# Block-sparse attention and a gated MLP: nine loads moved to GpSimd's queue, three transposes moved to the DMA, two weight transposes moved to later slots

## The chip, the cores and the metric

The kernel runs on one core of a Trainium2 chip. A core has five engines with a queue each: TensorE (PE) multiplies matrices, and its weight loads are listed apart as PEld; VectorE (DVE), ScalarE (ACT) and GpSimd (POOL) compute elementwise; SyncE (SP) issues transfers. Sixteen DMA engines move the data. TensorE writes to PSUM, and DVE or ACT take results from there to SBUF. Every engine works through its own instructions in order and waits on semaphores for the others. The metric is the device time of one execution in microseconds; given is the median of several runs.

## The reference

```python
# q, k, v: (4, 8, 768, 64); blocks of 32; window 1; first and last block global;
# three sampled blocks for each query block
scores = q @ k.T / sqrt(64)
scores = where(mask, scores, -1e9)
attn = softmax(scores)
x = (attn @ v), heads laid side by side            # (4, 768, 512)

h = relu(x @ w_in)                                 # (4, 768, 1024)
u, v = h[..., :512], h[..., 512:]
v_n = (v - mean(v)) / sqrt(var(v) + 1e-6)          # over the 512
v_s = einsum('ts,bsd->btd', w_spatial, v_n) + b_spatial
out = (u * v_s) @ w_out                            # (4, 768, 512)
```

Inputs and output are float32. The kernel computes in bfloat16 with float32 sums.

## The kernel before

Heads are taken in pairs: 16 pairs, four of them to a batch element. For a pair, k, q and v are loaded as float32 (`load`, line 105), cast to bfloat16 by POOL (`cast`, L138; k and q go into a tile `nat`, v into `vv`), and k and q are transposed. For pairs 0 to 3 PE transposes them; from pair 4 on SP issues one DMA transpose of the whole `nat` into `tt` (`tr_dma`, L448), and two DVE copies (`split`, L221, `kq<-tt`) bring the halves to the two heads' `kq`. The mask is part of the product: 24 more rows of `kq` hold one-hot blocks of keys and the bias of the query block.

Time is cut into slots, and the code at the end of the kernel (line 881 on) writes the order out by hand. In each slot PE computes one group of scores, ACT takes the exponential of it (L483 or L495), PE multiplies an earlier group with v, and then come the functions that are entered for this slot: `when(slot, ...)` enters them before the steps of the MLP, `late` behind these. Slots 0 to 35 do pairs 0 to 3 in thirds of the queries (`UNITS`, `qk_unit`, `av_unit`); from slot 36 on each slot is a sixth of one head (`qk_full`, `av_full`), so that a pair takes 12 slots, pair 4 from slot 36, pair 5 from 48, pair 6 from 60, pair 7 from 72.

The result of a unit is normalized by DVE (`normalize`, L506 and L507) into a tile `xn`. The MLP needs it transposed, `xt`. For pairs 0 to 3 `xtr_third` (line 564) does it third by third: two PE transposes (L308) into an unused part of the unit's own PSUM tile, and a DVE copy to `xt`. `XT_AT` gives the slots of these calls, otherwise 3u + 7 for unit u; units 8, 9, 10 and 11 are the last thirds of pairs 0 to 3. From pair 4 on a DMA transpose does it (`xtr_dma`, L573).

The MLP of a batch element is a list of steps, each one matmul of 512 columns (L621), dealt out over the slots by `run_queue` and the table `STEPS`: v and u products (x times `w_in`), s products (spatial weights times normalized v, evicted at L694), o products (times `w_out`). They write to two PSUM banks in turn. A v product is evicted by DVE (L188, `vn<-ps_moe`), its mean and variance taken by DVE (L657, L658), POOL makes `std` and `rstd` of a group (L661, L663), and DVE applies them (L188, `vn<-vn,mv,rstd`). In batch element 0 the groups are pairs of chunks: v0 and v1, v2 and v3, v4 and v5, and its v4 needs the last third of x of pairs 0 to 3, from slot 42 on.

The spatial weights are loaded by SP, cast by POOL in six parts at slots 19 to 29 (`ws_cast`, L589, into two buffers `ws_b`), and transposed by three DMA transposes (`ws_tr`, L593). `O_ACT` says which o products of each batch element ACT evicts and which DVE. SP's queue holds nearly all loads, stores and DMA transposes, in order.

Of the kernel before, what the change touches and what calls it, by code (L numbers as in the profile page):

```python
# [26 lines left out]
def kernel(  # L27
# [16 lines left out]
    nc = tc.nc  # L44
# [19 lines left out]
    TC = NCH // NT  # L64
    TW = TC * 128
# [152 lines left out]
    PL, DV = nc.gpsimd, nc.vector  # L218

    def dve_copy(o, i):  # L220
        nc.vector.tensor_copy(out=o, in_=i)  # L221
# [82 lines left out]
    def bank(nm="ps", tag=None):  # L304
        return psum.tile([128, 1024], BF16, tag=tag or moe_tag(), bufs=2 if tag else 1, name=nm)

    def tr(ps, c, in_):
        nc.tensor.transpose(out=ps[:, c * 128:(c + 1) * 128], in_=in_, identity=ident)  # L308

    def pair_of(src, c):  # L310
        return src[:, c].rearrange("p h d -> p (h d)")
# [143 lines left out]
    a_ref, av_ref, x_ref, xn_ref, xt_ref = {}, {}, {}, {}, {}  # L455
# [96 lines left out]
    def xt_tile(p):  # L552
        if p not in xt_ref:
            xt_ref[p] = work.tile([128, S], BF16, tag="xt", bufs=7, name="xt")
        return xt_ref[p]

    def xtr_pe(p, xn, c0, n, ps=None):
        if ps is None:
            ps = bank()
        for c in range(n):  # L560
            tr(ps, c, pair_of(xn, c))
        dve_copy(xt_tile(p)[:, c0 * 128:(c0 + n) * 128], ps[:, 0:n * 128])

    def xtr_third(u):
        t, p = UNITS[u]
        if t == "h":
            if p == 1:
                xtr_pe(0, xn_ref.pop(0), 0, 2 * TC)
        else:
            xtr_pe(p, xn_ref.pop(u), t * TC, TC, x_ref.pop(u))  # L570

# [54 lines left out]
        return out  # L626

    NORM_AT = {1: 23, 0: 23, 3: 36, 2: 36}
    O_ACT = [(4,), (0, 2, 4), (0, 2)]
    ST_ACT = [(), (), (4,), (0, 1, 2)]  # L630
    VN_AGE, VN_STEP = 9, 2
    post = []
# [1 line left out]
    class Moe:  # L634
# [75 lines left out]
        def o_product(self, tcc):  # L710
# [4 lines left out]
            for i in range(parts):  # L715
                cs = slice(i * w, (i + 1) * w)

                def done(ps, i=i, cs=cs):
                    if i == 0:
                        osb["t"] = work.tile([128, DM], FP32, tag="osb", bufs=6, name="osb")  # L720
                    on_act = (tcc + i) % 2 == 0 if self.last else tcc in O_ACT[self.b]
                    (act_copy if on_act else dve_copy)(osb["t"][:, cs], ps)
# [48 lines left out]
    def when(slot, *fns):  # L771
        at.setdefault(slot, []).extend(fns)

    def c(f, *a, **kw):
        return lambda: f(*a, **kw)
# [14 lines left out]
    when(2, staged)  # L790
    for p, sl in ((3, 18), (0, 21)):
        when(sl, c(tr_rest, p, 2 if p == 0 else 1))
    XT_AT = {1: 12, 3: 15, 5: 23, 11: 41}
    for u in range(1, len(UNITS)):
        late.setdefault(XT_AT.get(u, 3 * u + 7), []).append(c(xtr_third, u))
    late[12].append(c(tr_rest, 1))
# [54 lines left out]
    def slot_of(p):  # L851
        return S0 + 12 * (p - NG)

    for p in range(NG, NP):
        g = slot_of(p)
        when({4: 13, 5: 22, 6: 31}.get(p, g - 34), c(load, p, "k"), c(load, p, "q"), c(load, p, "v"))
        when({4: 18, 5: 26, 6: 38}.get(p, g - 24),
             c(cast, p, "k", PL), c(cast, p, "q", PL), c(cast, p, "v", PL))
        when({4: 20, 5: 31}.get(p, g - (16 if p in (10, 14) else 20)), c(tr_dma, p))
        when(31 if p == 4 else g - (7 if p in (9, 13) else 5), c(split, p, 0))  # L860
        when(32 if p == 4 else g - 3, c(split, p, 1))
        when(g + (18 if p == NP - 1 else 19 if p % NG == NG - 1 else 20), c(xtr_dma, p))
        if p == NP - 1:
            when(g + 20, last_x)
    for i, (ld, ca) in enumerate([(16, 19), (16, 21), (17, 23), (17, 25), (18, 27), (18, 29)]):
        if i < 5:
            when(ld, c(ws_load, i, 2 if i == 4 else 1))
        when(ca, c(ws_cast, i))
    for i, sl in enumerate((23, 27, 31)):
        when(sl, c(ws_tr, i))  # L870
    when(44, c(w_out_load, 0), c(w_out_load, 1), c(w_out_load2, 2))
    when(52, *[c(w_out_cast, g, PL) for g in range(NDH)])
# [58 lines left out]
```

## Time and profile before

| | |
|---|---|
| median of 3 runs | 208.85 us (208.24 to 209.13) |
| the profiled execution | 208.44 us, of which the span shown is 206.7 us |
| PE busy | 201.2 us |
| ACT busy | 166.8 us |
| DVE busy | 131.4 us |
| POOL busy | 74.4 us |
| moved by DMA | 42.41 MB, 205 GB/s |

A line of a timeline is: start, duration, engine, line and operation, output<-inputs, shapes, count, and in brackets the idle time of the engine just before it with what ended it. A line of the waits is: engine, line and output, what it waited for, total us, times, longest us. L12 is line 12 of the kernel. DMA-issuing instructions stand on the issuing engine with the time that the issue takes, and the time to landing counts from the issue. Times are microseconds from the start of the span.

### The profile page before, as it was taken

How to read it: one execution, taken by the hardware profiler on the slowest of the kernel's cores; microseconds unless marked ns; L12 is line 12 of the kernel's file. 1: busy time of each engine (PE TensorE's matmuls, PEld its weight loads, DVE VectorE, ACT ScalarE, POOL GpSimd, SP SyncE). 2: the span in 40 equal slices, each digit the busy share in tenths (PEclk: the TensorE clock that was granted, in tenths of full speed). 3: DMA queues.
4: the chain of work that ended last, by engine and by line, in shares of the span. 5: the costliest groups of instructions: out<-in, count | busy, mean ns of one | idle time of the engine just before them, and what ended most of it. 6: DMA issues, size and time to landing. Idle time of an engine off the chain costs nothing.

```text
span 206.7 us, 5245 instructions
## 1 busy us (share of the span) xinstructions
PE 201.2 (97%) x2122; PEld 126.4 (61%) x2122; DVE 131.4 (64%) x287; ACT 166.8 (81%) x222; POOL 74.4 (36%) x116
## 2 busy tenths in 40 slices
PE   8899999999999999999999999999999999999993
PEld 6679878766666666655655556655565656444441
DVE  7588797989654363648797355448686444576542
ACT  6999999999999999889999887998989883166021
POOL 6799799574680413210716401300202000013000
PEclk9999999999999999999999999999999999999999
DMA  5999999999999989999986749985101062960266
GB/s 140 355 362 359 326 410 270 235 250 333 267 357 201 251 242 203 325 308 271 285 113 172 174 89 264 205 236 127 38 3 38 0 92 51 162 235 0 44 163 251
DMA packets 66363, 42.41 MB, mean 205 GB/s; under 512 B 47524, under 2 KB 61220, under 8 KB 66340
## 3 DMA queue, kind: packets, MB, share of 16 engines
q1 hardware_dynamic: 65332, 40.71, 78.2%
q10 hardware_dynamic: 1008, 1.38, 1.8%
q8 instruction: 16, 0.26, 0.5%
q14 instruction: 7, 0.06, 0.1%
HBM read 24.38 MB, written 6.29 MB: 148 GB/s over the span
## 4 chain that ended last, share of the span: by engine, by line
PE 92%; DMA 3%; DVE 2%; SPq 1%; issue 0%; ACT 0%; ACTq 0%
PE ps_moe L621 33%; PE ps L491 23%; PE ps_av L542 13%; PE ps_t L621 8%; PE ps L478 6%; PE ps_sc L621 5%; PE ps_av L524 4%; DMA st_v<-in_v_dram 3%; DVE kq L221 1%; SPq L110 1%; PE ps L308 1%; PE ps_av L308 1%; DVE vv L138 1%; SPq L143 0%; DVE xn L507 0%
## 5 line engine op out<-in xcount | busy, mean ns | idle before, releaser
L495 ACT ACTIVATE a_all<-ps 128x768 bf16<-128x768 f32 x144 | 112.6, 812 | 11.7 <-PE ps L491 5.2
L491 PE MATMUL ps<-kq 88*128 88x384 bf16 x288 | 70.4, 325 | 0.0
L542 PEld LDWEIGHTS <-a_all 128*128 128x128 bf16 x864 | 45.2, 97 | 20.0
L542 PE MATMUL ps_av<-vv,a_all 128*128 128x65 bf16 x864 | 49.8, 193 | 0.0
L491 PEld LDWEIGHTS <-kq 88*128 88x128 bf16 x288 | 27.9, 97 | 29.0
L621 PE MATMUL ps_moe<-w_in_t,xt 128*128 128x512 bf16 x144 | 43.2, 378 | 0.0
L483 ACT ACTIVATE a_all<-ps 128x1024 bf16<-128x1024 f32 x36 | 34.0, 1026 | 1.5 <-PE ps L478 1.3
L621 PE MATMUL ps_moe<-vn,w_spt 128*128 128x512 bf16 x108 | 33.5, 378 | 0.0
L661 POOL TENSOR_SCALAR std<-mv 128x3 f32<-128x3 f32 (+1 forms) x9 | 2.9, 317 | 69.4 <-DVE mv L658 54.8
L138 POOL CAST nat<-st_k 128x768 bf16<-128x768 f32 (+2 forms) x18 | 13.8, 769 | 31.5 <-DMA st_k<-in_k_dram 30.4
L694 DVE SCALAR_TENSOR_TENSOR un<-ps_moe,b_col,un 128x512 bf16<-128x512 f32 x18 | 13.5, 749 | 14.8 <-PE ps_moe L621 14.8
L478 PE MATMUL ps<-kq 88*128 88x256 bf16 (+3 forms) x140 | 21.6, 275 | 1.2 <-DVE kq L221 0.5
L506 DVE RECIPROCAL rc<-ps_av 128x6 f32<-128x6 f32 (+1 forms) x36 | 6.7, 185 | 24.7 <-PE ps_av L542 23.2
L621 PEld LDWEIGHTS <-xt 128*128 128x128 bf16 x192 | 15.5, 98 | 7.8 <-issue 0.2
L507 DVE TENSOR_TENSOR xn<-ps_av,rc 128x384 bf16<-128x384 f32 (+1 forms) x36 | 18.5, 513 | 1.2
L621 PE MATMUL ps_moe<-w_out_t,gt 128*128 128x512 bf16 x60 | 18.1, 378 | 0.0
L657 DVE BATCH_NORM_STATS2 stats<-vn 128x6 f32<-128x512 bf16 x24 | 16.4, 684 | 1.3 <-ACT vn L652 0.9
L138 POOL CAST nat<-st_q 128x768 bf16<-128x768 f32 (+2 forms) x21 | 14.9, 708 | 3.8 <-DMA st_q<-in_q_dram 3.3
L478 PEld LDWEIGHTS <-kq 88*128 88x128 bf16 (+1 forms) x140 | 12.6, 97 | 5.6 <-DVE kq L221 1.6
L221 DVE COPY kq<-tt 64x1536 bf16<-64x1536 bf16 x24 | 15.1, 630 | 0.4
L188 DVE TENSOR_SCALAR vn<-ps_moe 128x512 bf16<-128x512 f32 x18 | 12.4, 686 | 4.7 <-PE ps_moe L621 4.6
L621 PEld LDWEIGHTS <-w_spt 128*128 128x128 bf16 x144 | 11.7, 98 | 5.2
(86 smaller groups left out, 208.1 us busy)
## 6 DMA issues: line engine op xcount, KB each, us to landing
st_v<-in_v_dram SPq DMA_DIRECT2D x16, 384.0 KB, 5.9
st_k<-in_k_dram SPq DMA_DIRECT2D x15, 384.0 KB, 5.0
out_dram<-osb SPq DMA_DIRECT2D x19, 256.0 KB, 2.7
st_q<-in_q_dram SPq DMA_DIRECT2D x12, 384.0 KB, 4.7
w_f<-in_moe_w_in_dram SPq DMA_DIRECT2D x6, 256.0 KB, 6.7
ws_f<-in_moe_w_spatial_dram SPq DMA_DIRECT2D x4, 384.0 KB, 7.5
out_dram<-osb ACTq DMA_DIRECT2D x4, 256.0 KB, 2.3
st_q<-in_q_dram SPq DMA_DIRECT2D x6, 128.0 KB, 5.6
```

The source lines that it names most:

```text
L138: eng.tensor_copy(out=dst, in_=src)
L188: nc.vector.tensor_scalar(out=out, in0=in0, scalar1=s1, scalar2=s2, op0=o0, **kw)
L221: nc.vector.tensor_copy(out=o, in_=i)
L478: nc.tensor.matmul(out=ps[:, at:at + n * TW], lhsT=kq[0:kr, h, ci * 128:(ci + 1) * 128], rhs=kq[0:kr, h, qcols(t0, n)], start=True, stop=True)
L483: nc.scalar.activation(out=out, in_=ps, func=AF.Exp, scale=0.125)
L491: nc.tensor.matmul(out=ps[:, hf * 512:hf * 512 + HALF], lhsT=kq[0:KR, j % H, ci * 128:(ci + 1) * 128], rhs=kq[0:KR, j % H, S + hf * HALF:S ...
L495: nc.scalar.activation(out=a_ref["h", j][:, ci, :].rearrange("p (b c) -> p b c", b=2), in_=ps.rearrange("p (b c) -> p b c", b=2)[:, :, 0:H ...
L507: nc.vector.tensor_tensor(out=out, in0=ps[:, :, 0:D], in1=rc[:, 0:n].to_broadcast([128, n, D]), op=ALU.mult)
L542: nc.tensor.matmul(out=av_ref[j][:, qc, 0:VA], lhsT=a_ref["h", j][:, ci, qc * 128:(qc + 1) * 128], rhs=vv[p % NVV][:, h, ci, 0:VA], start= ...
L621: nc.tensor.matmul(out=ref["ps"][:, 0:w], lhsT=lhs(i), rhs=rhs(i), start=(i == 0), stop=(i == n - 1))
L657: nc.vector.bn_stats(out=stats, in_=self.vn[:, tcc, :])
L694: nc.vector.scalar_tensor_tensor(out=self.un[:, tcc, :], in0=ps, scalar=b_col[:, tcc:tcc + 1], in1=self.un[:, tcc, :], op0=ALU.add, op1=AL ...
```

## The change

Five edits. The loads of k, q and v of pairs 5, 6 and 7 are issued by POOL (`nc.gpsimd`), the others of this loop by SP as before; pair 6's are entered at slot 27 where they were at slot 31. For units 8, 9 and 10, `xtr_third` issues a DMA transpose from SP in place of the two PE transposes and the DVE copy, at slots 29, 32 and 35 where they were at 31, 34 and 37. The transpose of pair 5's k and q moves from slot 31 to 33. The DMA transposes of the second and third parts of the spatial weights move from slots 27 and 31 to 39 and 41. One eviction of an o product in each of batch elements 0 and 1 moves from ACT to DVE.

```diff
         if t == "h":
             if p == 1:
                 xtr_pe(0, xn_ref.pop(0), 0, 2 * TC)
+        elif t == 2 and p < 3:
+            nc.sync.dma_start_transpose(
+                out=xt_tile(p)[:, t * TW:(t + 1) * TW].rearrange("p (c n) -> p c n", c=TC),
+                in_=xn_ref.pop(u).rearrange("p c h d -> p (c h d)"))
         else:
             xtr_pe(p, xn_ref.pop(u), t * TC, TC, x_ref.pop(u))
...
-    O_ACT = [(4,), (0, 2, 4), (0, 2)]
+    O_ACT = [(), (0, 2), (0, 2)]
...
-    XT_AT = {1: 12, 3: 15, 5: 23, 11: 41}
+    XT_AT = {1: 12, 3: 15, 5: 23, 8: 29, 9: 32, 10: 35, 11: 41}
...
-        when({4: 13, 5: 22, 6: 31}.get(p, g - 34), c(load, p, "k"), c(load, p, "q"), c(load, p, "v"))
+        when({4: 13, 5: 22, 6: 27}.get(p, g - 34),
+             *[c(load, p, nm, eng=PL if 4 < p < 8 else nc.sync) for nm in "kqv"])
...
-        when({4: 20, 5: 31}.get(p, g - (16 if p in (10, 14) else 20)), c(tr_dma, p))
+        when({4: 20, 5: 33}.get(p, g - (16 if p in (10, 14) else 20)), c(tr_dma, p))
...
-    for i, sl in enumerate((23, 27, 31)):
+    for i, sl in enumerate((23, 39, 41)):
         when(sl, c(ws_tr, i))
```

In the order of the instructions of the changed kernel, POOL's queue has pair 5's loads between the second and third L589 casts, pair 6's loads right behind pair 5's casts and ahead of the last two L589 casts, and pair 7's loads behind pair 6's casts. SP's queue has, from pair 4's transpose on: the first spatial transpose, x of unit 8, x of unit 9, pair 5's transpose, x of unit 10, the second spatial transpose, pair 6's transpose, the third spatial transpose, then the loads of `w_out`.

## The prediction

> **What bounds the kernel now.** I read the page's busy table and its chain, then TensorE's waits, then busy time by stage.
>
> ```profile
> span 206.7 us, 5245 instructions
> ...
> PE 201.2 (97%) x2122; PEld 126.4 (61%) x2122; DVE 131.4 (64%) x287; ACT 166.8 (81%) x222; POOL 74.4 (36%) x116
> ...
> PE 92%; DMA 3%; DVE 2%; SPq 1%; issue 0%; ACT 0%; ACTq 0%
> ```
>
> ```profile
> PE wps L182 <- DVE past L162: 1.0, 1, 1.0
> PE ps L478 <- DVE kq L221: 0.5, 2, 0.4
> PE ps L478 <- ACT a_all L483: 0.5, 1, 0.5
> ```
>
> ```profile
> 35.00:40.00 5.00, 5.00 (x76) 4.03 (x73) 4.93 (x9) 4.85 (x6) 3.74 (x4) 1.00 1.33 292
> 40.00:45.00 5.00, 5.00 (x57) 3.10 (x56) 4.38 (x13) 5.00 (x8) 3.81 (x4) 1.00 0.96 194
> ...
> 50.00:172.00 122.00, 122.00 (x1317) 74.34 (x1314) 71.63 (x143) 110.50 (x149) 31.50 (x41) 1.00 0.80 186
> ```
>
> The columns of the stages are the stretch, its length, then busy us of PE, PEld, DVE, ACT and POOL, the granted clock, the DMA share and GB/s. PE is the bound: 92% of the chain, 2.0 us of waits in the whole span, 122.00 of 122.00 us busy from 50 to 172. Since a matmul's end is modelled, busy alone proves little; the distance between starts does.
>
> ```profile
> 46.27 0.65 PE ps_moe L621 x3
> ...
> 49.10 0.43 PE ps_moe L621 x2
> ...
> 175.92 1.29 PE ps_moe L621 x6
> ```
>
> A 512-column matmul takes 0.65/3 = 0.217 us at 46 and 1.29/6 = 0.215 us at 176, when ACT and DMA load PE little. So PE runs at its own pace all along. Two things follow. The most that can be gained is the PE work removed. And a stall of PE is paid in full at the end, since no later stretch has room to win it back. In 35 to 40, where the change lies, DVE is also full (4.93 of 5).
>
> **What the change costs, part by part.** *Transposes of x.* Three calls at line 570 (the last third of pairs 0, 1, 2) leave PE and DVE.
>
> ```profile
> 39.36 0.28 PE L308 MATMUL ps_av<-ident,xn 128*128 128x128 bf16 x2
> 39.47 0.60 PE L478 MATMUL ps<-kq 88*128 88x256 bf16 x4
> ...
> 40.94 0.38 PE L621 MATMUL ps_moe<-w_in_t,xt 128*128 128x512 bf16 x1
> ```
>
> One pair of transposes moves PE by 39.47 - 39.36 = 0.11 us, three by 0.33 us: the whole possible gain. Three DVE copies go too; they also release their PSUM bank earlier. In their place SP issues three DMA transposes.
>
> *Nine loads.* k, q and v of pairs 5, 6 and 7 leave SP and enter POOL's queue. SP saves about nine times 0.49 us, worth nothing while PE waits for no load.
>
> ```profile
> 31.51 0.49 SPq L110 DMA_DIRECT2D st_q<-in_q_dram  x1
> ...
> 39.13 2.89 SPq L448 DMA_TRANSPOSE tt<-nat  x1
> ```
>
> The cost is on POOL, which runs in order. By the order of the changed kernel, pair 5's loads stand between the second and the third cast of the spatial weights (L589), ahead of std and rstd (L661, L663); pair 6's stand behind pair 5's casts, ahead of the last two L589 casts and the next std and rstd.
>
> ```profile
> 28.89 4.61 POOL L589 CAST ws_b<-ws_f 128x768 bf16<-128x768 f32 x3
> ...
> 33.89 0.72 POOL L663 TENSOR_TENSOR rstd<-std,mhalf 128x2 f32<-128x2 f32 x1
> 34.58 1.56 POOL L589 CAST ws_b<-ws_f 128x768 bf16<-128x768 f32 x1
> 36.19 0.83 POOL L138 CAST nat<-st_k 128x768 bf16<-128x768 f32 x1
> ...
> 38.19 0.83 POOL L138 CAST vv<-st_v 128x768 bf16<-128x768 f32 x1
> 41.02 3.08 POOL L589 CAST ws_b<-ws_f 128x768 bf16<-128x768 f32 x2 [2.00 <-DMA w_spt<-ws_b]
> ...
> 44.50 0.73 POOL L663 TENSOR_TENSOR rstd<-std,mhalf 128x2 f32<-128x2 f32 x1
> ```
>
> POOL shows no pause from 28.89 to 39.02. So three loads that hold POOL for T each shift the first rstd from 34.61 to 34.61 + 3T. No row of before has a load on POOL. From below, T is an SP issue, 0.49 us; from above the longest POOL row of this stretch, 1.57 us (4.61/3 is 1.54, one alone is 1.56). Below nothing is excluded: no POOL work is removed. I take 0.83 us, the same engine's cast of the same tile, as the nearest row; so 3T = 2.5 us. The Trainium skill, page "DMA: Bandwidth & Descriptors", section "Latency and other measured facts", puts the first byte of a GpSimd-issued DMA at about 1 us against about 0.6 for one from SP; no row here shows it, and as an estimate with T = 1.0 the sum below would be +2.2 us.
>
> Who waits for rstd: DVE, in order, at the first vn.
>
> ```profile
> 35.08 1.22 DVE L188 TENSOR_SCALAR vn<-vn,mv,rstd 128x512 bf16<-128x512 bf16 x1
> ...
> 38.18 0.27 DVE L221 COPY xt<-ps_av 128x256 bf16<-128x256 bf16 x1
> 38.38 0.16 DVE L506 RECIPROCAL rc<-ps_av 128x4 f32<-128x4 f32 x1
> 38.57 0.42 DVE L507 TENSOR_TENSOR xn<-ps_av,rc 128x256 bf16<-128x256 f32 x1
> ...
> 39.51 0.68 DVE L188 TENSOR_SCALAR vn<-ps_moe 128x512 bf16<-128x512 f32 x1
> ...
> 45.46 0.41 DVE L188 TENSOR_SCALAR vn<-vn,mv,rstd 128x512 bf16<-128x512 bf16 x1
> ...
> 47.08 0.67 DVE L188 TENSOR_SCALAR vn<-ps_moe 128x512 bf16<-128x512 f32 x1
> ```
>
> ```profile
> L188 DVE TENSOR_SCALAR vn<-vn,mv,rstd x24: 379/408/1218, 35.1 to 190.3; 128x512 bf16<-128x512 bf16 x24
> ```
>
> That vn took 1.22 us where the median is 0.408, and ended at 36.30, just after POOL's cast of 34.58 ended (36.14); it follows POOL there, so DVE's stream shifts by the whole 3T. Behind it stand both splits of pair 4, two normalizations and the eviction of v2 (39.51 to 40.19). That eviction frees the PSUM bank which u2's first product takes at 40.94. The removed copy gives 38.38 - 38.18 = 0.20 us back. Net delay of PE: 40.19 - 0.20 + 3T - 40.94 = 3T - 0.95, or +1.5 us. It is measured against the old start, so the transposes removed by then are in it.
>
> *The x by DMA.* SP is in order: x of pair 1's third, then pair 5's transpose (slot 33), then x of pair 2's third. Pair 1's xn is done at 38.57 + 0.42 - 0.20 + 3T. The issue of a third I scale from L573, which issues three times as much in 1.25 us: 0.42, with 0 and 1.25 as ends.
>
> ```profile
> L573 SPq DMA_TRANSPOSE xt<-xn x12: 1210/1246/1831, 59.6 to 176.9; - x12
> ...
> DMA to landing us min/median/max: 2.7/3.7/5.8
> ```
>
> Pair 5's transpose then starts at 39.2 + 3T, holds SP 2.89 us, and pair 2's third is issued at 42.1 + 3T. For its landing the ends are 2.7 and 5.8; I take 3.3, below the median 3.7 because it is a third of the size, above the least because it stands right behind a large transpose: 45.4 + 3T. PE wants it at v4's third matmul, the second of the three at 46.27: 46.49. So its delay is 3T - 1.1 = 1.4 us: as late as the bank, and paid once with it. At a landing of 5.8 it would be 3T + 1.4.
>
> *The second rstd.* It ends in before at 45.23, 2.00 us of which is POOL waiting for the weights' DMA, which the new order has behind it by then. After: 45.23 - 2.00 + 6T = 48.2. DVE asks at 45.46 + 1.5 = 47.0 and waits 1.2 us; the next that PE needs from it is v4's eviction (47.08 to 47.75), for u4's first product, the second matmul of the two at 49.10 (49.32). The cover is 1.57 us, so it costs nothing; without the cover 1.2 us.
>
> *The rest.* Weights 2 and 3 go to SP at slots 39 and 41, and land some 6 to 10 us later than before.
>
> ```profile
> 65.67 0.74 DVE L694 SCALAR_TENSOR_TENSOR un<-ps_moe,b_col,un 128x512 bf16<-128x512 f32 x1
> ...
> 88.28 0.59 ACT L224 ACTIVATE osb<-ps_moe 128x512 f32<-128x512 f32 x1
> ...
> 88.70 0.20 DVE L506 RECIPROCAL rc<-ps_av 128x6 f32<-128x6 f32 x1 [1.70 <-PE ps_av L542]
> ```
>
> The second weights serve the product that is evicted at 65.67, so they are wanted after about 62; issued near 45 they have some 10 us to spare. Two evictions move from ACT to DVE: DVE was idle 1.70 us up to 88.70, where the first (ACT, 0.59 us at 88.28) would fall, so it costs DVE up to 0.7 us beside PE and PE nothing. Pairs 6 and 7 reach their transposes 2 to 4 us later; their first use is more than that behind.
>
> **Sum.** The profiled execution took 208.44 us, its span 206.7 and 1.7 around it. 208.44 + 1.5 = 209.9. The median of the three runs is 208.85, 0.4 above that execution, and I forecast on the median: 210.35, say 210.4.
>
> **The rivals.** *Not slower: the loads are cheap on POOL.* The place is the same bank at 40.94. With T = 0.49 the sum is 3 x 0.49 - 0.95 = +0.5 us, 209.4; under T = 0.32 nothing of it reaches PE, and only the 0.33 us of transposes are left, 208.5. For it: SP's row for the same transfer. Against it: POOL has no pause there, and DVE none. Within 0.5% of before (1.04 us, about what a measurement of this kernel can tell from no change) it stays up to T = 0.66.
>
> *Both rstd are late: the loads hold POOL for longer.* At T = 1.57 the first delay is 3.8 us; the second rstd ends at 43.23 + 9.4 = 52.7, DVE asks at 49.2, and of 3.4 us some 1.9 are left beyond the cover: +5.6 us, 214.5. DVE's second wait is 43.23 + 6T - (45.46 + 3T - 0.95) = 3T - 1.28; it passes the cover of 1.57 from T = 0.95 on, and I count this rival from T = 1.2, +3.4 us. For it: vn at 35.08, three times its median beside a POOL cast, so the two engines hold each other up. The Trainium skill, page "SBUF — State Buffer", section "Who interferes with whom", has the rule: VectorE operations in a two-port mode and GpSimd exclude each other, and descriptors of GpSimd's DMAs wait for the lock. The trace agrees by that 1.22 against 0.408 us. Against it: between 32 and 35 DVE reads mostly PSUM.
>
> *x comes late by itself.* A landing of 5.8 us gives 3T + 1.4 = +3.9 us, 212.7; x thirds would be the last to come at 46.5.
>
> *Faster by over 0.5%* needs 1.04 us; the removed PE work is 0.33 us. Only a pace of PE other than in before would do it.
>
> **How the numbers follow.** Forecast (T from 0.66 to 1.2, +1.0 to +3.4 us): 0.45. Cheap loads: 0.36. Both rstd: 0.12. Late x: 0.05. Faster: 0.02. So slower 0.62, same 0.36, faster 0.02. The range goes from the cheap end, 208.4, to between late x and both rstd, 213.6. The forecast's own range is 209.8 to 212.2.
>
> **What would show it.** Rows of DMA issues on POOL at 32 to 35 and 39 to 42, with their length T; the first rstd ending near 37; idle of DVE before L188 put down to POOL rstd, some 2 us; waits of PE at L621 on DVE vn near 41 to 43, and on the x transposes near 48, of which the waits of before have neither; PE's work three pairs of transposes less; the attention of pair 5 on starting 1.5 us later. The prediction is wrong if T is well under 0.5 us, if POOL takes up later work while descriptors are written, or if PE shows idle elsewhere, as at pair 6's or 7's splits.

## The result, and the profile after

The changed kernel takes 218.2 us (median of 6 runs, 216.16 to 224.34), the kernel before 208.5 us beside it (6 runs, 207.76 to 209.13): 1.044 times as long, 95% interval 1.041 to 1.047. That is 9.7 us by these medians and 9.2 us by the ratio. Two of the six runs, the profiled one among them, are in a slower state, and every ratio here leaves such runs out. The forecast was 210.4 us, its range 208.4 to 213.6. The profiled execution took 221.0 us (span 219.2), so its stalls add up to some 3 us more than those of the median.

From the page of the changed kernel: span, busy time, the chain by engine.

```profile
span 219.2 us, 5247 instructions
...
PE 204.0 (93%) x2116; PEld 127.1 (58%) x2116; DVE 129.4 (59%) x286; ACT 166.5 (76%) x220; POOL 80.4 (37%) x125
...
PE 51%; DMA 2%; ACT 0%; issue 0%; ACTq 0%
```

PE was 97% busy and is 93%; the chain, 92% PE before, can be followed through only half of the span. From line 569 on, the kernel's line numbers that stand here are 4 higher than before (L625 was L621). PE's waits, then three of DVE's (what waited, on what, total us, times, longest):

```profile
PE ps_moe L625 <- DVE vn L188: 4.6, 3, 2.3
PE ps_av L308 <- DVE xn L507: 2.3, 1, 2.3
PE ps_moe L625 <- DVE osb L221: 1.3, 1, 1.3
...
PE ps_moe L625 <- DMA xt<-xn: 0.9, 1, 0.9
```

```profile
DVE vn L188 <- POOL rstd L667: 11.7, 4, 5.1
DVE kq L221 <- DMA tt<-nat: 8.1, 3, 3.5
...
DVE xn L507 <- DMA xt<-xn: 3.1, 1, 3.1
```

None of these waits of PE stands in its list of before. Taken from the distances between the starts of PE's matmuls, PE stands still for 0.5 us at 41.1, 2.5 at 47.5, 2.5 at 55.7, 2.1 at 65.5, 1.5 at 97.1 and 1.1 at 103.1, and runs at half pace from 47.7 to 50.8, which costs another 1.3: 11.5 of the 12.5 us by which the span is longer. (The 1.5 us at 97.1 are an eviction that stands on DVE behind a split; the split waited 3.48 us, until 95.2, for a DMA transpose of k and q.)

Where that comes from stands in POOL's timeline of the changed kernel (start, us, engine, line, operation; in brackets the idle time before):

```profile
31.76 0.95 POOL L110 DMA_DIRECT2D st_k<-in_k_dram  x1
32.71 0.75 POOL L110 DMA_DIRECT2D st_q<-in_q_dram  x1
33.44 0.73 POOL L110 DMA_DIRECT2D st_v<-in_v_dram  x1
...
36.15 0.73 POOL L667 TENSOR_TENSOR rstd<-std,mhalf 128x2 f32<-128x2 f32 x1
36.85 1.54 POOL L593 CAST ws_b<-ws_f 128x768 bf16<-128x768 f32 x1
42.43 0.83 POOL L138 CAST nat<-st_k 128x768 bf16<-128x768 f32 x1 [4.04 <-PE ps L491]
...
46.11 0.83 POOL L138 CAST vv<-st_v 128x768 bf16<-128x768 f32 x1 [1.71 <-DMA st_v<-in_v_dram]
...
52.55 0.73 POOL L667 TENSOR_TENSOR rstd<-std,mhalf 128x2 f32<-128x2 f32 x1
```

The loads hold POOL for 0.73 to 0.95 us each, as forecast. But POOL then stands at 38.4 before pair 5's casts, because their data are not there. The nat cast's wait is put down to PE, which had long been done; k landed at 42.31. The first rstd comes at 36.88 (forecast 37.1), the second at 53.27 (forecast 48.2). From the DMA view of 31 to 48 us: transfers by issuing queue, count, KB, median us to landing.

```profile
st_k<-in_k_dram POOLq DMA_DIRECT2D x2, 384.0 KB, 7.4
st_q<-in_q_dram POOLq DMA_DIRECT2D x2, 384.0 KB, 10.6
st_v<-in_v_dram POOLq DMA_DIRECT2D x1, 384.0 KB, 12.6
xt<-xn SPq DMA_TRANSPOSE x3, 9.6
w_spt<-ws_b SPq DMA_TRANSPOSE x2, 12.0
```

In before such loads landed in a median of 4.7 to 5.9 us, pair 5's in 5.2, 5.6 and 6.1, and the same weights' transpose, issued at 33.57, in 7.4. Now pair 5's k, q and v take 10.5, 10.8 and 12.6 us, the transpose issued at 31.85 beside them 12.3, the small x transpose of 35.04 11.9. The stages show it once more. First after, then before; the last three columns are granted clock, DMA share and GB/s.

```profile
35.00:42.00 7.00, 6.64 (x97) 5.03 (x94) 5.00 (x11) 6.63 (x9) 3.22 (x4) 1.00 1.13 134
42.00:48.00 6.00, 3.66 (x29) 1.86 (x26) 2.80 (x9) 4.07 (x6) 3.55 (x5) 0.93 1.13 197
```

```profile
35.00:42.00 7.00, 7.00 (x105) 5.48 (x103) 6.90 (x14) 6.85 (x9) 4.72 (x5) 1.00 1.22 263
42.00:48.00 6.00, 6.00 (x52) 3.41 (x50) 5.13 (x14) 6.00 (x9) 4.63 (x6) 1.00 1.02 269
```

The DMA share adds up the time of all packets, so it can pass 1. By it the DMA engines are nearly as busy as before (1.13 against 1.22), and they move half as much (134 against 263 GB/s).

### The profile page after: what moved, and what is told of

Read it like the earlier page. It is cut to its first block, busy times and chain, and to the rows that moved or that the text cites. A ratio compares the mean times of both kernels' runs of the same rounds, so it can differ in the third digit from the quotient of the medians.

```text
span 219.2 us, 5247 instructions
## 1 busy us (share of the span) xinstructions
PE 204.0 (93%) x2116; PEld 127.1 (58%) x2116; DVE 129.4 (59%) x286; ACT 166.5 (76%) x220; POOL 80.4 (37%) x125
## 4 chain that ended last, share of the span: by engine, by line
PE 51%; DMA 2%; ACT 0%; issue 0%; ACTq 0%
PE ps_moe L625 20%; PE ps L491 12%; PE ps_av L542 7%; PE ps_t L625 7%; PE ps_sc L625 5%; DMA xt<-xn 2%; ACT osb L224 0%; ACTq L224 0%
## 5 line engine op out<-in xcount | busy, mean ns | idle before, releaser
L491 PE MATMUL ps<-kq 88*128 88x384 bf16 x288 | 71.2, 328 | 0.1
L625 PE MATMUL ps_moe<-w_in_t,xt 128*128 128x512 bf16 x144 | 44.2, 383 | 3.6 <-DVE vn L188 2.7
L625 PE MATMUL ps_moe<-vn,w_spt 128*128 128x512 bf16 x108 | 33.5, 378 | 2.0 <-DVE vn L188 2.0
L625 PEld LDWEIGHTS <-xt 128*128 128x128 bf16 x192 | 15.6, 99 | 9.2 <-DMA xt<-xn 1.2
L698 DVE SCALAR_TENSOR_TENSOR un<-ps_moe,b_col,un 128x512 bf16<-128x512 f32 x18 | 13.5, 749 | 12.6 <-PE ps_moe L625 12.5
L188 DVE TENSOR_SCALAR vn<-vn,mv,rstd 128x512 bf16<-128x512 bf16 x24 | 12.5, 554 | 11.8 <-POOL rstd L667 11.7
L625 PE MATMUL ps_moe<-w_out_t,gt 128*128 128x512 bf16 x60 | 18.1, 378 | 1.3 <-DVE osb L221 1.3
L221 DVE COPY kq<-tt 64x1536 bf16<-64x1536 bf16 x24 | 13.3, 553 | 8.5 <-DMA tt<-nat 8.1
## 6 DMA issues: line engine op xcount, KB each, us to landing
st_q<-in_q_dram POOLq DMA_DIRECT2D x3, 384.0 KB, 10.3
```

What stands on the lines that cost most here:

```text
L188: nc.vector.tensor_scalar(out=out, in0=in0, scalar1=s1, scalar2=s2, op0=o0, **kw)
L491: nc.tensor.matmul(out=ps[:, hf * 512:hf * 512 + HALF], lhsT=kq[0:KR, j % H, ci * 128:(ci + 1) * 128], rhs=kq[0:KR, j % H, S + hf * HALF:S ...
L625: nc.tensor.matmul(out=ref["ps"][:, 0:w], lhsT=lhs(i), rhs=rhs(i), start=(i == 0), stop=(i == n - 1))
L698: nc.vector.scalar_tensor_tensor(out=self.un[:, tcc, :], in0=ps, scalar=b_col[:, tcc:tcc + 1], in1=self.un[:, tcc, :], op0=ALU.add, op1=AL ...
```

## The experiments

Three theories stood after the result. A: loads on a second queue and SP's DMA transposes, in flight together, make each other late; late loads hold POOL in front of rstd, rstd holds DVE, DVE holds PE. B: loads on GpSimd's queue are slow by themselves. C: the loss is in the other edits (x by DMA, the weights' transposes). All ratios are against the kernel before on the same chip.

**Which edits cost what.** The changed kernel with all nine loads back on SP:

```diff
-             *[c(load, p, nm, eng=PL if 4 < p < 8 else nc.sync) for nm in "kqv"])
+             *[c(load, p, nm, eng=nc.sync) for nm in "kqv"])
```

> The changed kernel with the nine loads back on SP's queue, at the slots of the change; x by DMA, the later weight transposes and the moved evictions stay. Theory A (the loads on a second queue run beside SP's DMA transposes, both land late, and the late landings hold POOL, DVE and PE): nearly all of the loss goes, 208 to 209.5 us, and no wait of PE over 0.5 us after 20 us. Theory B (GpSimd's descriptors make its own loads slow, whatever runs beside): the same. Theory C (the x by DMA and the later weight transposes are the loss): 214 us or more stays.

211.43 us, 1.015 [1.010, 1.019]: +3.0, where A had left at most 1.1. So 6.7 of the 9.7 us (by the ratios 6.1 of 9.2) go with the queue of the loads, 3.0 with the rest. What PE waits for in it:

```profile
PE ps_moe L625 <- DMA xt<-xn: 1.0, 1, 1.0
...
PE ps_av L308 <- DVE xn L507: 0.9, 1, 0.9
PE ps_moe L625 <- DVE osb L221: 0.7, 1, 0.7
```

The second is a buffer: `xn` of unit 11 takes one of three buffers again, that of unit 8, which a DMA transpose reads until 45.33, where PE had read it at once. The first lies at 94.6 and the third at 88.5, far from the change.

The kernel before with the loads of pairs 5 to 7 on POOL (pair 6 at slot 27) and nothing else:

```diff
-        when({4: 13, 5: 22, 6: 31}.get(p, g - 34), c(load, p, "k"), c(load, p, "q"), c(load, p, "v"))
+        when({4: 13, 5: 22, 6: 27}.get(p, g - 34),
+             *[c(load, p, nm, eng=PL if 4 < p < 8 else nc.sync) for nm in "kqv"])
```

> The kernel before with the loads of pairs 5 to 7 on POOL's queue, pair 6's at slot 27, and nothing else of the change. Theory A and B: most of the loss, 214 to 218 us, with landings of over 9 us for the loads of pairs 5 and 6. Theory C: 208 to 210.5 us.

218.74 us, 1.050 [1.045, 1.055]: the loads alone cost 10.3 us, as much as the whole change (the two intervals overlap). POOL's timeline, and PE's longest wait:

```profile
38.73 1.19 POOL L138 CAST nat<-st_k 128x768 bf16<-128x768 f32 x1 [0.21 <-DMA st_k<-in_k_dram]
46.05 0.83 POOL L138 CAST nat<-st_q 128x768 bf16<-128x768 f32 x1 [6.13 <-DMA st_q<-in_q_dram]
...
53.73 0.73 POOL L663 TENSOR_TENSOR rstd<-std,mhalf 128x2 f32<-128x2 f32 x1
```

```profile
PE ps_moe L621 <- DVE vn L188: 7.2, 1, 7.2
```

That is A's chain in one piece: q lands 13.2 us after its issue, rstd ends at 54.5, PE stands 7.2 us. C is not the main loss; by the kernel with the loads back on SP it is worth 3.0 us.

**Holding POOL against landing late.** The nine loads on SP, and in their places on POOL nine copies of about the same length, which hold POOL and move no data:

```diff
+    def hold():
+        nc.gpsimd.tensor_copy(out=lim, in_=hot)
...
+        if 4 < p < 8:
+            when({5: 22, 6: 27}.get(p, g - 34), hold, hold, hold)
```

> The changed kernel with the nine loads on SP's queue, and in their places on POOL nine copies of 128x768 bf16 from one unused tile to another, about as long as a load holds POOL (0.75 us). It shows the predicted term by itself. By the prediction (POOL held for 0.75 us each): 3 x 0.75 - 0.95 = +1.3 us over the same kernel without the copies. Theories A and B: this part is small beside the loss, 0.5 to 2 us of it. A rival by which POOL's hold alone makes the loss: 214 us or more.

212.21 us, 1.018 [1.015, 1.021]: 0.8 above the 211.43 without the copies, where the prediction's sum gives 1.3; the two intervals overlap, so even the 0.8 is hardly clear of the noise. The time that loads take on POOL, on which the whole forecast was built, is thus a small part of what goes with the queue; the other 5 to 6 us come with the late data.

**B: another second queue.** The loads on ACT's queue:

```diff
-             *[c(load, p, nm, eng=PL if 4 < p < 8 else nc.sync) for nm in "kqv"])
+             *[c(load, p, nm, eng=nc.scalar if 4 < p < 8 else nc.sync) for nm in "kqv"])
```

> The changed kernel with the nine loads on ScalarE's queue in place of POOL's: a second queue as well, but POOL isn't held and writes no descriptors. Theory A: the loads and the transposes beside them still land late (over 9 us) and the kernel takes 213 to 219 us. Theory B: landings of 5 to 7 us and 208 to 211 us, the ScalarE issue of nine times 0.34 us among it.

218.9 us, 1.052 [1.048, 1.056]. Pair 4's transpose now takes 11.8 us to land and the weights' 10.1 (6.9 and 7.4 before), so SP's transposes suffer from ACT's queue too. Pair 5's loads take 8.3 to 8.6 us, less than A had foreseen and more than B. The time itself decides little: PE waited 7.1 us for ACT's a_all, as ACT stood between its issues.

**C in single edits.** Only x of units 8 to 10 by DMA:

```diff
+        elif t == 2 and p < 3:
+            nc.sync.dma_start_transpose(
...
-    XT_AT = {1: 12, 3: 15, 5: 23, 11: 41}
+    XT_AT = {1: 12, 3: 15, 5: 23, 8: 29, 9: 32, 10: 35, 11: 41}
```

> The kernel before with the last third of x of pairs 0 to 2 by DMA at the slots of the change, and nothing else. By the prediction's step: 0 to -0.3 us, 208.1 to 208.5. By what the kernel with the loads put back showed (unit 11's normalization waits for the landing of unit 8's transpose, since three buffers serve the units; +3 us there): 209 to 211.5 us, with a wait of DVE at L507 on the transposes of x.

216.44 us, 1.038 [1.034, 1.042], more than either forecast: 8 us for an edit that is part of the 3.0 above. SP's timeline tells why.

```profile
44.95 3.32 SPq L597 DMA_TRANSPOSE w_spt<-ws_b  x1
48.37 2.48 SPq L570 DMA_TRANSPOSE xt<-xn  x2
```

With the weights at their old slots two of the x transposes stand behind the third weights' transpose, which waits for POOL's casts; PE waited 5.0 us for them. A rival was the buffer of `xn`; the same with these three tiles in a buffer of their own:

```diff
+                if t == 2 and p < 3:
+                    xn_ref[u] = lim.rearrange("p c n -> p (c n)")[:, p * TW:(p + 1) * TW].rearrange(
+                        "p (c h d) -> p c h d", h=2, d=D)
```

> The same, with the normalized thirds of units 8, 9 and 10 in an otherwise unused tile instead of the three buffers that the units share, so that unit 11 waits for no transpose. If that buffer is the cost of the x by DMA: 208.0 to 208.6 us and no wait of DVE at L507 on a DMA. If the landing of unit 10's x is (the prediction's place, v4's third product): 209 us or more with a wait of PE at the product on the x transposes.

216.47 us, 1.040 [1.035, 1.044]: the buffer is not it. Then x by DMA with the weights moved behind it:

```diff
-    for i, sl in enumerate((23, 27, 31)):
+    for i, sl in enumerate((23, 39, 41)):
```

> The kernel before with the three thirds of x by DMA and the second and third spatial weights' transposes moved to slots 39 and 41, loads on SP as before. If the 8 us that x by DMA cost by itself were SP's order (x waits behind a weights' transpose that waits for GpSimd's casts), x is now ahead, and 209.5 to 211.5 comes out, with no PE wait on the x transposes above 1.5 us. If the transposes of x land late anyway, 214 to 217.

211.7 us, 1.014 [1.008, 1.019]: SP's order it was, and the weights' later slots are what pays for x by DMA. PE still waits 1.6 us for one x transpose. Last the weights and the two evictions alone, on the kernel before:

```diff
-    O_ACT = [(4,), (0, 2, 4), (0, 2)]
+    O_ACT = [(), (0, 2), (0, 2)]
...
-    for i, sl in enumerate((23, 27, 31)):
+    for i, sl in enumerate((23, 39, 41)):
```

> The kernel before with the two evictions moved from ScalarE to VectorE and the second and third weight transposes at slots 39 and 41, and nothing else. By the prediction, which costed both at nothing: 208.2 to 208.8 us. If they cost by themselves (PE waited 0.7 to 1.3 us for an eviction by VectorE near 90 us in the changed kernel): 209 to 210 us with that wait.

209.16 us (10 runs), 1.005 [1.002, 1.007], with one new wait of PE, at 92.3 us:

```profile
PE ps_moe L621 <- DMA xt<-xn: 1.0, 1, 1.0
```

The x transpose of the second batch element is issued at 86.67 instead of 84.33: SP's queue, which runs in order, has not caught up 40 us after the weights were moved. So "the rest", costed at nothing, costs 1 us.

**Without the transposes beside them.** The loads alone (as in the second experiment) without the weights' transposes. `w_spt` is set to zero at the start instead, which delays PE's first product by 1.9 us.

```diff
+    nc.vector.memset(w_spt, 0.0)
...
-        nc.sync.dma_start_transpose(
-            out=w_spt[:, 2 * i:2 * i + 2].rearrange("p t c n -> p (t c) n"),
-            in_=ws.pop(("b", i)).rearrange("p t c s -> p (t c s)"))
+        ws.pop(("b", i))
```

> The kernel before with the nine loads on GpSimd's queue and without the three transposes of the spatial weights (they are left out, so the spatial product uses zeros in their place). If loads on a second queue are late because SP's transposes are in flight with them, pair 5's loads land in under 8 us (10 to 13.7 with the transposes there), the second rstd comes before 48, and 209 to 212.5 comes out. If GpSimd's queue is late by itself, landings stay at 10 us or more and 216 to 219 comes out.

211.59 us, 1.015 [1.010, 1.019], about 209.7 without the delay at the start. Pair 5's loads land in 5.2, 5.5 and 5.7 us, and POOL never waits for them. POOL's timeline, then PE's longest wait (the one at the start):

```profile
37.98 0.82 POOL L138 CAST nat<-st_k 128x768 bf16<-128x768 f32 x1
38.75 0.83 POOL L138 CAST nat<-st_q 128x768 bf16<-128x768 f32 x1
...
48.55 0.73 POOL L662 TENSOR_TENSOR rstd<-std,mhalf 128x2 f32<-128x2 f32 x1
```

```profile
PE mq L316 <- DVE bm L189: 1.9, 1, 1.9
```

B falls: on the same queue, in the same places, the loads are on time once the weights' transposes are gone. With it falls the rival that DVE, at work beside POOL as before, holds up the loads that POOL issues. But it is not any transpose that does the harm: in this kernel pair 6's loads (issued from 40.35 on) run beside pair 5's transpose (issued at 39.60), and they land in 5.9 to 6.4 us, the transpose in 7.0.

**Where the late data bite.** Pair 5's casts behind the second rstd (slot 37), its transpose at slot 38:

```diff
-        when({4: 18, 5: 26, 6: 38}.get(p, g - 24),
+        when({4: 18, 5: 37, 6: 38}.get(p, g - 24),
...
-        when({4: 20, 5: 33}.get(p, g - (16 if p in (10, 14) else 20)), c(tr_dma, p))
+        when({4: 20, 5: 38}.get(p, g - (16 if p in (10, 14) else 20)), c(tr_dma, p))
```

> The changed kernel with pair 5's three casts moved behind the second rstd on GpSimd (slot 26 to 37, and pair 5's transpose from 33 to 38). If the late landings cost time because the casts that wait for them stand ahead of rstd, the second rstd ends near 48 instead of 53.3, VectorE's wait of 5.1 us falls under 2, PE's gap of 2.46 us near 55.7 goes, and 2 to 4 us of the 9.7 are won: 214.5 to 216.5. If VectorE's wait for rstd is not what sets PE, 217.5 to 219.

1.042 [1.036, 1.049]: the steps came as expected, the time did not. The second rstd ends at 47.7 and DVE's waits for rstd fall from 11.7 to 2.8 us. The late data now hold pair 5's transpose and DVE's split instead, and x still comes late (its transposes land after 9.9 to 12.0 us). DVE's waits in this kernel, then PE's:

```profile
DVE kq L221 <- DMA tt<-nat: 6.5, 2, 5.5
...
DVE vn L188 <- POOL rstd L667: 2.8, 2, 1.7
```

```profile
PE ps_av L308 <- DVE xn L507: 2.7, 1, 2.7
PE ps_moe L625 <- DMA xt<-xn: 1.2, 1, 1.2
```

DVE's 5.5 us at the split reach PE with 0.4. What costs PE here is x: 2.7 and 1.2 us of waits, and behind the first of them half pace from 47.6 to 54.5, with a granted clock of 0.50 to 0.52, which costs some 3 us more.

Pair 5 on SP, pairs 6 and 7 on POOL; then the reverse:

```diff
+             *[c(load, p, nm, eng=PL if p in (6, 7) else nc.sync) for nm in "kqv"])
...
+             *[c(load, p, nm, eng=PL if p == 5 else nc.sync) for nm in "kqv"])
```

> The changed kernel with pair 5's loads back on SP; pairs 6 and 7 stay on GpSimd's queue. If the loss is pair 5's loads that run beside the weights' first transpose, most of the 9.7 us goes: 211.5 to 214 (211.4 with all nine loads on SP, plus up to 0.8 per three loads that hold GpSimd). If every pair on GpSimd's queue costs alike, 215 to 217.

> The changed kernel with only pair 5's loads on GpSimd's queue; pairs 6 and 7 on SP. If pair 5's loads beside the weights' first transpose are the loss, 215 to 218, with the second rstd after 50. If every pair costs alike, 212.5 to 214.

1.036 [1.029, 1.043] and 1.037 [1.034, 1.040]. So not pair 5 alone: each set by itself costs 4 to 5 us over the 211.43 with all on SP, and together not the sum, but 6 to 7. In the one PE waits for an x transpose that was beside pair 6's loads, in the other for the xn buffer held by the x transpose beside pair 5's. PE's longest wait in the one and in the other:

```profile
PE ps_moe L625 <- DMA xt<-xn: 3.8, 1, 3.8
```

```profile
PE ps_av L308 <- DVE xn L507: 4.2, 1, 4.2
```

Last, the changed kernel with the weights' first transpose some 4 us behind pair 5's loads:

```diff
-    for i, sl in enumerate((23, 39, 41)):
+    for i, sl in enumerate((32, 39, 41)):
```

> The changed kernel with the first spatial weights' transpose at slot 32 instead of 23, which puts it on SP behind the x transpose of pair 0's third, some 4 us behind pair 5's loads on GpSimd's queue. If the two at once are the loss, pair 5's loads land in 5 to 9 us instead of 10.5 to 12.6, the second rstd ends at 48 to 49.5 instead of 53.3, and 213 to 216.5 comes out. If the loads are late without it, 217 to 219.

215.91 us, 1.031 [1.024, 1.038]. Pair 5's loads land in 4.2, 4.5 and 6.3 us and the second rstd ends at 47.4: with the first weights' transpose moved away from them, and the same data moved in sum, they are on time on POOL's queue. The next collision then decides: pair 6's loads, issued from 41.0 on, beside pair 5's transpose (8.9 us) and x (issued 43.78), for which PE waits 3.8 us.

**The mix by itself.** Five runs without any computation (outputs zero) put three loads of 128x768 f32 on one queue beside 128x1536 transposes on SP.

> A kernel that computes nothing (its output is zeros): ten groups of transfers, each started only when the last group has landed. Loads are three of 384 KB as for a pair, transposes are of 128x1536 bf16 as for pair 5. Groups: loads on SP; loads on POOL; one transpose; one transpose and loads on SP behind it; beside it on POOL; beside it on ScalarE; then two transposes alone, with loads behind on SP, beside on POOL, beside on ScalarE. Theory A (a second queue beside transposes is what makes both slow): loads on POOL alone land within 1.5 us of those on SP; beside transposes the transposes land 3 us or more later than alone, and the whole group with two queues takes 2 us or more longer than on one queue; POOL and ScalarE alike. Theory B (GpSimd's own loads are slow): POOL's loads alone already need 8 us or more, and ScalarE's group is as fast as SP's.

> No computation at all here (the output is zeros, so its time stands for nothing but itself): groups of 2 or 4 transposes of a 128x1536 bf16 tile on SP, and about 3 us after the first of them three loads of 128x768 f32 on GpSimd's queue, on ScalarE's, or on SP's; two groups also keep VectorE copying bf16 tiles in SBUF (one of them with loads on GpSimd's queue and no transpose). If two queues that work at once are what makes both late, loads on GpSimd's and on ScalarE's queue land alike, some 7 to 10 us after issue beside four transposes, and 5 to 6 us without any. If GpSimd's own queue is slow, its loads land 2 us or more later than ScalarE's beside the same transposes. If busy VectorE is what holds GpSimd's queue up, the last group (no transpose, copies) lands at 8 us or more instead of about 6. If none of these, all loads land in 5 to 7 us, and the 10 to 13 us of the changed kernel need something that these groups lack.

> No computation again (output zeros). Each group gives SP four loads and a transpose as a backlog, then two more transposes, while three loads start on another queue at about the moment when the backlog ends: on GpSimd's queue, on ScalarE's, and, for comparison, all on SP in order; then GpSimd's without the two later transposes, GpSimd's a little later and a little earlier, and GpSimd's beside a VectorE that copies without pause. If loads and transposes that run at once on two queues move less in sum, the groups with two queues take 3 us or more longer from first issue to last landing than the one on SP alone, single loads land after 8 to 13 us, and the recorded rate falls to some 100 to 150 GB/s where either alone has about 300; without the later transposes the loads land in under 7 us. If only GpSimd's queue does this, ScalarE's group is like SP's. If the kernel's own traffic is needed, all groups take the same time within 1.5 us, except the last.

> The mix of loads on GpSimd's queue and transposes on SP's again (output zeros), alone, beside a stream of 512-column products on TensorE, beside ScalarE's copies, VectorE's, GpSimd's, all four together, then all four with the loads on SP in order, and alone once more. If other engines' traffic makes the 10 us, a group with it lands its loads after 9 us or more, where the group alone has 4.4 to 6.4, and the one on SP stays at 4 to 6. If traffic does not matter, all mixed groups land within 1.5 us of the first, and the two groups alone show the scatter.

> The mix without computation (output zeros), nine times: SP's queue takes four, two or no loads as a backlog and then four transposes; three loads go to GpSimd's queue behind none, one or two casts of 0.8 us, so that they start with the backlog, with the first transpose, or behind it. If the moment decides, a group whose loads and transposes start within 1 us of each other lands its loads after 9 us or more and its second transpose after 7 or more, where other groups stay under 8. If it does not, all loads land in 4 to 8 us, and the cause of the kernel's 10 to 13 us stays open.

Read from the traces, issue to landing in us:

```
                                             k    q    v     transposes
loads alone, SP / POOL                      3.2/3.8, 3.8/4.0, 4.1/4.5   (one transpose alone 3.7)
1st mix: POOL's loads, 1 transpose          3.6  5.4  5.6    6.5
2nd: POOL's / ACT's 5 us behind two         3.7/3.5, 3.9/4.2, 4.6/4.6   3.9 4.2 / 3.8 4.1
2nd: POOL's / ACT's at the last of four     5.3/4.8, 5.6/5.4, 5.9/5.8   (the last one 6.0 / 6.2)
2nd: POOL's beside VectorE copying only     3.5  4.1  4.5
3rd: POOL's / ACT's among three             4.4/4.1, 6.1/5.8, 6.4/6.2   6.2 4.5 7.0 / 6.1 4.7 6.6
4th: POOL's, all four engines busy          5.2  5.5  5.7    6.9 5.8 6.8
5th: loads 5 us ahead of the transposes     3.8  3.9  5.6    7.9 5.1 3.9 4.3
5th: loads and third transpose at 58.4      5.7  7.4  11.1   5.1 4.0 12.7 12.1
```

The first four missed the size. ScalarE's queue does much as GpSimd's. With two queues a group of the third took 16.3 to 17.0 us where SP alone did the same work in 14.7, though its loads also started some 3 us later. With all four engines busy the loads took 5.2 to 5.7 us, alone 4.7 to 5.6, so other engines' traffic does not make the 10 us. In one group of the fifth, loads and a transpose were issued at one moment behind a backlog, as in the kernel: the last load took 11.1 us and the transposes beside it 12 to 13, with nothing else on the chip. The DMA view of that group (57.5 to 72.5; packets and rate, then the transposes' median us to landing), then of the group with the loads ahead:

```profile
DMA packets 5817, 2.55 MB, mean 170 GB/s; under 512 B 5529, under 2 KB 5577, under 8 KB 5817
...
tt<-nat SPq DMA_TRANSPOSE x3, 12.1
```

```profile
DMA packets 7696, 4.33 MB, mean 222 GB/s; under 512 B 6384, under 2 KB 7456, under 8 KB 7696
...
tt<-nat SPq DMA_TRANSPOSE x4, 4.7
```

The group took 21.6 us against 18.2. The two groups move the same data. Four other groups of this run, issued 0.3 to 1.2 us apart but with two loads or none as backlog, had loads in 4.2 to 7.8 and transposes in up to 9.5, so the moment alone does not decide. Nor does the backlog: in the third run loads and a transpose were issued 0.1 us apart behind the same four loads, and they landed in 4.4 to 7.0. The kernel's delays came out without computation in this one group, once; what sets their size stays open.

The Trainium skill, page "DMA: Bandwidth & Descriptors", section "Issuing engines are not separate DMA queues", says that transfers from all issuing engines run on the same 16 DMA engines and interleave. The runs agree, and show more: interleaved loads and transposes moved less in sum than one behind the other (21.6 us against 18.2). The Trainium skill, page "DMA: Bandwidth & Descriptors", section "Queues, rings and completion order", has each DMA engine go round its queues packet by packet. That would fit the packets seen in the changed kernel, where those of the loads (4608 bytes) took a mean of 471 ns and up to 2.2 us in 32 to 44, when a typical one took 205.

The queue is not all that the move changes. In these traces a load of k, q or v goes mostly in packets of 4608 bytes on POOL's queue and of 1536 bytes on SP's and ACT's. The larger packets are not needed for the harm, as the kernel with the loads on ACT's queue shows by its transposes; whether they add to it was not tried. Why the interleaving costs throughput was not tried either and stays open. No version here beat the kernel before.

## Why the prediction was wrong, by its own steps

- *PE is the bound and a stall is paid in full.* Right: 11.5 us of stalls and slow pace are 11.5 of 12.5 us of span, and no later stretch won anything back.
- *T, a load's hold on POOL, 0.83 us.* Right: 0.95, 0.75 and 0.73, so 3T is 2.43 (taken 2.5). First rstd 36.88, forecast 37.1.
- *The bank freed by v2's eviction, 3T - 0.95 = +1.5.* The place is right, the size is not. PE stood 0.5 us there; counted against the old start, as the prediction does, the product came 41.13 - 40.94 = 0.2 us later. DVE starts vn 1.83 us later, but the work behind it is quicker, since POOL now stands still: the split behind it takes 0.54 us (before, beside POOL's casts, 1.21) and the second vn 0.40 (0.90). DVE's timeline of the changed kernel:

```profile
36.91 1.64 DVE L188 TENSOR_SCALAR vn<-vn,mv,rstd 128x512 bf16<-128x512 bf16 x1 [1.90 <-POOL rstd L667]
38.47 0.54 DVE L221 COPY kq<-tt 64x1536 bf16<-64x1536 bf16 x1
38.94 0.40 DVE L188 TENSOR_SCALAR vn<-vn,mv,rstd 128x512 bf16<-128x512 bf16 x1
```

- *The second rstd, 45.23 - 2.00 + 6T = 48.2, its wait under the cover.* This step failed, and with it the forecast. The sum has no term for pair 5's casts waiting for their data: it took the landings as they were on one queue. They came after 10.5 to 12.6 us, rstd at 53.27, and the cover of 1.57 us stood against a wait of 5.06. On it, and on the same once more at pair 6's loads (rstd at 64.97), hang 4.6 of PE's 11.5 us. With the loads moved and the weights' transposes left out, some 209.7 us came out.
- *x by DMA: landing 3.3 us, ends 2.7 and 5.8, issue of a third 0.42.* Failed likewise: the ends were rows of a trace in which no loads ran on another queue beside the transposes. They landed after 11.9 and 7.3 us; with all loads on SP it was 6.9, 5.3 and 2.7. An issue took 1.17 to 1.50 us, about as long as one three times as large (1.21 to 1.77): the scaling was wrong. "Paid once with the bank" was wrong too: x came in through the buffer of `xn`, which the prediction did not name, 2.5 us at 47.5, and the half pace of 1.3 us behind it.
- *The rest costs nothing.* Wrong by 1.0 us, as the weights' slots and the evictions showed by themselves: the slack of 10 us was counted for the weights, not for what stands behind them on SP.
- *The rivals.* "Both rstd are late" had the right place and PE's right wait, but for a reason that the runs exclude (T from 1.2 on); 214.5 us was still 3.7 short. That the loads' time on POOL costs little is what the cheap rival gave and the copies showed, at some 0.8 us, but with T near 0.8 and not at 0.49.

## What to carry to other kernels

A second queue was no free lane beside several DMA transposes: where loads move off the queue that orders them, ask what will be in flight with them, and take no landing time from a trace in which that never happened. Put nothing that others wait for behind a cast of freshly loaded data on an in-order engine, and do not expect much when only this is mended: with the casts moved, the late landings came out at the split and at x. When a transpose goes from PE to DMA, count the longer life of its source buffer and everything behind it on SP.

## What was not expected of the hardware

Loads and transposes on two queues, started together, moved 134 GB/s in 35 to 42 with the DMA engines as busy as at 263. A DMA transpose of 128x256 holds SP for 1.17 us or more. And PE's clock: after the stall of 2.5 us at 47.5 it ran at half pace for 3 us (384 columns in 0.320 us instead of 0.163), but not after the stalls of 2.5 at 55.7 and 2.1 at 65.5. The granted clock is the third number from the end.

```profile
45.00:50.00 5.00, 2.66 (x15) 1.43 (x15) 1.22 (x3) 2.23 (x4) 3.89 (x5) 0.71 0.92 150
50.00:55.00 5.00, 3.35 (x31) 1.77 (x30) 1.69 (x4) 2.78 (x4) 3.89 (x5) 0.94 1.34 170
55.00:60.00 5.00, 4.35 (x49) 2.75 (x49) 4.74 (x10) 3.41 (x5) 0.83 (x1) 1.00 0.61 92
```

The Trainium skill, page "TensorE: Matmul & The Clock Gate", section "Part 1: The HAM clock gate", puts the window of this clock at some 3.4 us; the half pace of the changed kernel lasted about that long (3.1 us), that of the kernel with the casts moved twice as long (6.9). In the changed kernel a stall shorter than the window was enough once out of three times.
